# An mLSTM scan with its feed-forward on one core: scores of the first six chunks from each head's own 40 rows, in two halves of the array by turns, and a new list of first steps

## The chip, the cores and the metric

One NeuronCore of a Trainium2 chip. A kernel's time is the device time of one launch, in microseconds, the median of three runs. What is profiled is one execution of its own, whose time stands beside its span below.

## The reference, cut to what matters

```python
# q, k, v, o_gate: (4, 8, 768, 40); i_gate, f_gate: (4, 8, 768)
for t in range(S):
    m_new = maximum(f[t] + m, i[t]);  f_stab = exp(f[t] + m - m_new);  i_stab = exp(i[t] - m_new)
    C = f_stab * C + i_stab * outer(v[t], k[t])          # (40, 40) of each head
    n = f_stab * n + i_stab * k[t]
    y[t] = sigmoid(o_gate[t]) * (C @ q[t]) / maximum(abs(n . q[t]), 1.0)
x = y.transpose(0, 2, 1, 3).reshape(3072, 320)
h = x @ w_in                                             # (320, 2048)
g = maximum(h, 0) + alpha * minimum(h, 0)
out = g @ w_out                                          # (2048, 320)
```

## The kernel before, in words

The scan is done in chunks of 128 tokens, 24 in all (4 sequences of 6), with the 8 heads of a chunk together. A chunk's output is the sum of two products: its tokens among themselves, where the scores k.q of a head (128x128) are weighed with decays and multiplied with the values, and the state C of all earlier chunks, multiplied with q. Two chunks make a group of 256 tokens, on which the feed-forward runs: up with `w_in` (`ph`, lines 738 to 745), an activation, a split into a high and a low part (`gh`, `gl`), and down with `w_out` (`po`, line 775).

The first six chunks (`NDIR = 6`, one sequence) take another way than the rest: their products are float32. The step `qTn`/`kTn` turns q and k of a chunk by a transpose on TensorE into `pqk`, with two heads in one column block of 128: the even head of a pair in rows 0 to 39, the odd head in rows 64 to 103 (`R = 64 + D` = 104 rows). `qcn` copies q out of PSUM in one copy (`qf`, line 1034). `kcn` copies k twice, by `padded_copy`: rows 0 to 63 into the first half of `kf` (line 330), rows 64 to 103 into the second half (line 331). The other rows of both halves of the two `kf` tiles hold zeros, written once by the step `kfz` (`padded_tiles`, lines 319 and 320, GpSimd). The scores of the even heads (`sc n 0`) and of the odd heads (`sc n 1`) are then two steps of four matmuls each over all 104 rows, where the zeros take the other head out (`scores`, line 1102). `wg n par` weighs such a half with its decays on VectorE (`weigh`, line 1106), `v n` multiplies with the values (`values`, line 351), `fm n` is the product with the state (`pI`, line 412), `um n` the chunk's own addition to the state (`pu`, line 193).

Beside this the opening loads both weight matrices. Each comes as 64-bit words over SP's queue and is made into float32 on chip: the step `d` of a block issues the load (`wi`, `wr`, `wo`), `s`, `x`, `y`, `j` put the words together on ScalarE and VectorE (lines 834 to 858), `h`/`H` cast the high part on ScalarE and `k`/`K` on GpSimd (line 866), `l`/`L` take the low part on VectorE and `p` on GpSimd (line 870). Blocks are `i00` to `i31` (rows of `w_in`), `r0`, `r2` (its last 64 rows) and `o0` to `o7` (`w_out`). `warm2` issues two matmuls of 256 columns whose result nobody reads (`dense`, line 166).

What sets the order of all this is the string `ORDER`: names of steps, run one after the other; `pin` then ties every instruction behind the one that was issued before it on its engine, so no scheduler moves anything. `dqn`, `dvn`, `don`, `dLn` in it issue the loads of q and k, v, the output gate and the decays. After the names of `ORDER` come those of `PATTERN`, group by group, to the end; `U`, `R`, `S`, `G`, `K`, `D` are the steps of a feed-forward piece (up, relu, activation, high, low, down).

Transposes, scores and updates take their PSUM tiles by turns from four buffers (`psa`); the first chunks' scores borrow the feed-forward's.

Of the kernel before, what the change touches and what calls it, by code (L numbers as in the profile page):

```python
# [17 lines left out]
def kernel(ctx: ExitStack, tc: tile.TileContext, q, k, v, i_gate, f_gate, o_gate, w_in, w_out, alpha, out):  # L18
    nc = tc.nc
# [6 lines left out]
    halves = slice(0, P // 2), slice(P // 2, P)  # L26
# [14 lines left out]
    turns = ["b", "a"]  # L41

# [270 lines left out]
    kpads = []  # L313
# [328 lines left out]
    def row_of(g, fp, e):  # L642
# [302 lines left out]
    def first_group():  # L945
# [78 lines left out]
        for j in range(2):  # L1024
            kpads.append(sb.tile([P, 2, 512], F32, tag="kS", name=f"kf{j}", bufs=2))
# [67 lines left out]
        def scores(n, par):  # L1093
            if n >= GC:
                ps = psa(f"pS{n}_{par}")
            elif n * par == 0:
                ps = ps_h.tile([P, 512], F32, tag="h", name=f"pS{n}_{par}")
            else:
                ps = ps_o.tile([P, 512], F32, tag="o1", name=f"pS{n}_{par}")
# [97 lines left out]
        def decay_parts(k, tag):  # L1197
# [29 lines left out]
            kfz=padded_tiles, Cz=zero_states,  # L1227
# [5 lines left out]
        def values_of(n):  # L1233
            got["h", n] = values(n, [E[n, 0], E[n, 1]])
# [5 lines left out]
        def chunk_steps(n):  # L1240

            steps[f"wd{n}"] = lambda: weighed(n)
            steps[f"v{n}"] = lambda: values_of(n)
# [9 lines left out]
            for par in range(2):  # L1253
# [5 lines left out]
                steps[f"sc{n}{par}"] = lambda par=par: scores(n, par)  # L1259
# [115 lines left out]
```

## Time and profile before

| | |
|---|---|
| median of 3 runs | 455.18 us (455.04 to 455.19) |
| the profiled execution | 454.57 us |
| its span, first to last instruction | 452.7 us |
| PE busy | 445.0 us (98%) |
| DVE / ACT / POOL busy | 307.4 / 313.7 / 310.0 us |
| chain that ended last, by engine | PE 88%, ACT 3%, DMA 2%, DVE 2%, issue 2% |
| the six chunks' scores (line 1102), busy | 13.0 us in 96 instructions |

A float32 matmul shows as two instructions in the profile, so four matmuls of a score step are "x8". An instruction's time holds some 0.17 us in which the next one already runs; what a step costs the engine is read from the distance of two starts or from the chain of waits, where each piece is counted once. The opening is the stretch to about 113 us in which the first two groups' feed-forward is mixed with the chunks and the weights; behind it the order is that of `PATTERN`.

### The profile page before, as it was taken

Reading aid. Unit: us, or ns where it says so; the run is one execution under the profiler, and the core shown is the slowest. Engines: PE = TensorE matmul, PEld = TensorE weight load, DVE = VectorE, ACT = ScalarE, POOL = GpSimd, SP = SyncE. Lnnn points to the kernel's source line nnn. Section 1 sums busy time; section 2 is a strip of 40 time slices with the busy share of each in tenths; the row PEclk is TensorE's granted clock in tenths of the full one; section 3 lists DMA queues with packets and bytes.
Section 4 is the critical chain, followed back from the end, with each engine's and each line's share of the span. In section 5 each row is a group of like instructions: output and inputs, shape, how many; then the busy total and the mean of one; then the engine's idle time right before and its main releaser. Section 6 shows DMA issues by size and latency. Waiting matters only on the chain.

```text
span 452.7 us, 12026 instructions
## 1 busy us (share of the span) xinstructions
PE 445.0 (98%) x4560; PEld 433.4 (96%) x4560; DVE 307.4 (68%) x659; ACT 313.7 (69%) x717; POOL 310.0 (68%) x400
## 2 busy tenths in 40 slices
PE   8999999999999999999999999999999999999997
PEld 6779999999999999999999999999999999999996
DVE  4799999557866867767768767758758757753321
ACT  5999997858857867758858758659759658433331
POOL 7846366667879689588798698597798696143241
PEclk9999999999999999999999999999999999999999
DMA  8998996289875575596773774598572451000000
GB/s 186 220 261 204 284 237 203 52 165 225 183 162 113 134 167 109 129 178 165 152 165 96 134 177 104 112 192 178 128 179 77 98 140 41 2 30 0 30 1 29
DMA packets 156163, 61.61 MB, mean 136 GB/s; under 512 B 140154, under 2 KB 145834, under 8 KB 156106
## 3 DMA queue, kind: packets, MB, share of 16 engines
q1 hardware_dynamic: 156026, 60.75, 59.1%
q8 instruction: 36, 0.59, 0.5%
q14 instruction: 21, 0.17, 0.1%
q10 hardware_dynamic: 80, 0.11, 0.1%
HBM read 36.90 MB, written 4.03 MB: 90 GB/s over the span
## 4 chain that ended last, share of the span: by engine, by line
PE 88%; ACT 3%; DMA 2%; DVE 2%; issue 2%; POOL 1%; SPq 1%; POOLq 0%; DVEq 0%
PE po L775 36%; PE ph L738 5%; PE ph L743 5%; PE ph L739 5%; PE ph L740 5%; PE ph L745 5%; PE ph L741 5%; PE ph L742 5%; PE ph L744 5%; PE pH L392 4%; PE pS L494 4%; PE pu L193 1%; PE pI L418 1%; PE px L603 1%; DMA kn<-in_k_dram 1%
## 5 line engine op out<-in xcount | busy, mean ns | idle before, releaser
L764 POOL TENSOR_TENSOR gl<-g,gh 128x512 fp32r<-128x512 f32 x74 | 95.7, 1294 | 32.6 <-ACT gh L762 31.4
L775 PE MATMUL po<-OH,gh 128*128 128x320 f32 x368 | 111.5, 315 | 0.0
L748 ACT ACTIVATE g<-ph 128x512 f32<-128x512 f32 x96 | 57.4, 598 | 76.7 <-PE ph L745 74.8
L775 PE MATMUL po<-OL,gh 128*128 128x320 f32 x368 | 108.7, 308 | 0.0
L753 DVE SCALAR_TENSOR_TENSOR g<-g,oma,ph 128x256 f32<-128x256 f32 x148 | 63.6, 471 | 65.1 <-ACT g L748 65.0
L775 PEld LDWEIGHTS po<-OH,gh 128*128 128x128 f32 x368 | 69.2, 188 | 0.0
L775 PEld LDWEIGHTS po<-OL,gh 128*128 128x128 f32 x368 | 69.2, 188 | 0.0
L775 PE MATMUL po<-OH,gl 128*128 128x320 f32 x368 | 68.7, 308 | 0.0
L775 PEld LDWEIGHTS po<-OH,gl 128*128 128x128 f32 x368 | 57.5, 188 | 0.0
L738 PE MATMUL ph<-XH,WH 128*128 128x256 f32 x192 | 54.1, 282 | 0.3 <-ACT wi L844 0.3
L739 PE MATMUL ph<-XH,WH 128*128 128x256 f32 x192 | 53.3, 278 | 0.0
L743 PE MATMUL ph<-XL,WH 128*128 128x256 f32 x192 | 53.1, 277 | 0.1
L740 PE MATMUL ph<-XH,WL 128*128 128x256 f32 x192 | 53.2, 277 | 0.0
L745 PE MATMUL ph<-XL,W 128*128 128x256 f32 x192 | 53.1, 277 | 0.0
L741 PE MATMUL ph<-XH,WL 128*128 128x256 f32 x192 | 53.1, 277 | 0.0
L742 PE MATMUL ph<-XH,W 128*128 128x256 f32 x192 | 53.0, 276 | 0.0
L744 PE MATMUL ph<-XL,WH 128*128 128x256 f32 x192 | 53.0, 276 | 0.0
L377 ACT CAST E<-pS 128x512 bf16<-128x512 f32 x72 | 41.1, 582 | 15.1 <-DVE pS L374 15.1
L465 ACT ACTIVATE E<-Lb,gates 128x128 f32<-128x128 f32 x160 | 50.0, 392 | 0.0
L762 ACT CAST gh<-g 128x512 fp32r<-128x512 f32 x74 | 45.7, 618 | 4.0 <-PE po L775 2.4
L738 PEld LDWEIGHTS ph<-XH,WH 128*128 128x128 f32 x192 | 36.0, 188 | 0.6 <-ACT wi L844 0.4
L450 POOL TENSOR_TENSOR og<-og,r 128x320 f32<-128x320 f32 x18 | 13.0, 724 | 34.3 <-DVE r L443 32.8
(200 smaller groups left out, 1126.1 us busy)
## 6 DMA issues: line engine op xcount, KB each, us to landing
Lb<-L_d SPq DMA_DIRECT2D x20, 512.0 KB
wo<-in_moe_w_out_dram SPq DMA_DIRECT2D x8, 640.0 KB
wi<-in_moe_w_in_dram SPq DMA_DIRECT2D x8, 512.0 KB
qn<-in_q_dram SPq DMA_DIRECT2D x24, 160.0 KB
kn<-in_k_dram SPq DMA_DIRECT2D x24, 160.0 KB
og<-in_o_gate_dram SPq DMA_DIRECT2D x24, 160.0 KB
va<-in_v_dram SPq DMA_DIRECT2D x24, 160.0 KB
out_dram<-ob SPq DMA_DIRECT2D x11, 320.0 KB
```

The source lines that it names most:

```text
L738: nc.tensor.matmul(dst, WH[half][:, 0, hs], XH[:, 0], start=True, stop=False)
L739: nc.tensor.matmul(dst, WH[half][:, 1, hs], XH[:, 1], start=False, stop=False)
L740: nc.tensor.matmul(dst, WL[half][:, 0, hs], XH[:, 0], start=False, stop=False)
L741: nc.tensor.matmul(dst, WL[half][:, 1, hs], XH[:, 1], start=False, stop=False)
L742: nc.tensor.matmul(dst, W2[:, fs], XH[:, 2], start=False, stop=False)
L743: nc.tensor.matmul(dst, WH[half][:, 0, hs], XL[:, 0], start=False, stop=False)
L744: nc.tensor.matmul(dst, WH[half][:, 1, hs], XL[:, 1], start=False, stop=False)
L745: nc.tensor.matmul(dst, W2[:, fs], XL[:, 2], start=False, stop=True)
L748: nc.scalar.activation(gt, ph, AF.Relu, scale=-1.0)
L753: nc.vector.scalar_tensor_tensor(out=y[:, e], in0=gt[:, e], scalar=oma[:, f : f + 1], in1=ph[:, e], op0=ALU.mult, op1=ALU.add)
L764: (nc.vector if split else nc.gpsimd).tensor_tensor(gl, y, gh.bitcast(F32), ALU.subtract)
L775: nc.tensor.matmul(po[j], x[:, e, j * P : (j + 1) * P], W[f // NB][:, f % NB], **ends)
```

## The change

The scores of a chunk become one step `scn`. Each of its matmuls reads only the 40 rows of one head: rows 0 to 39 of `qf` and `kf` for the even head of a pair, rows 64 to 103 for the odd one, and the two alternate, pair by pair, into two PSUM tiles. In the built program those matmuls have a tile of 64x128 of the array, at row 0 and at row 64; before they had 128x128. `kf` needs no zeros: `kfz`, `padded_tiles` and `padded_copy` go, and `kcn` is one copy of 104 rows as `qcn` is. `ORDER` is written anew: 20 steps `warm2` more (90 filling matmuls in place of 50), the casts `i00h`, `r0h`, `o2h`, `i30h`, `o7h` now on GpSimd (`k`), `i11k` now on ScalarE (`h`), `o7l` on GpSimd (`p`), and most names at other places. The steps from `PATTERN` are as before. A loop that only reserved buffers a second and a third time goes as well.

```diff
-    def padded_tiles():
-        for K in kpads:
-            nc.gpsimd.memset(K[64:R, 0], 0.0)
-            nc.gpsimd.memset(K[:64, 1], 0.0)
...
-    def padded_copy(K, pk):
-        nc.scalar.copy(K[:64, 0], pk[:64])
-        nc.scalar.copy(K[64:R, 1], pk[64:R])
...
-    ORDER = """warm14 dq0 Cz warm2 warm2 warm2 qT0 warm2 sca0 lf0a kT0 i00d lf0z lf0b li0 L0 sca1 bj0 dq1 warm2 qc0 lqa lqb kc0
+    ORDER = """warm14 dq0 Cz i00d qT0 lf0z sca0 dq1 lf0a warm2 lf0b warm2 L0 warm2 lqa dv0 sca1 i00s warm2 warm2 kT0 sp01 warm2
...
+        keys = [sb.tile([P, 2, 512], F32, tag="kS", name=f"kf{j}", bufs=2)[:, 0] for j in range(2)]
...
             if j == 0:
-                qk[n] = sb.tile([P, 512], F32, tag="qf", name=f"qf{n}"), padded(n)
-                copy(qk[n][j][:R], pq[:R])
-            else:
-                padded_copy(qk[n][j], pq)
+                qk[n] = sb.tile([P, 512], F32, tag="qf", name=f"qf{n}"), keys[(n + NDIR) % 2]
+            copy(qk[n][j][:R], pq[:R])
...
-        def scores(n, par):
-            if n >= GC:
-                ps = psa(f"pS{n}_{par}")
...
+        def scores(n):
+            for par in range(2):
+                if n >= GC:
+                    ps = psa(f"pS{n}_{par}")
...
+                pS[n, par] = ps
             for p in range(NPR):
                 sl = slice(p * P, (p + 1) * P)
-                nc.tensor.matmul(ps[:, sl], qk[n][1][:R, par, sl], qk[n][0][:R, sl], start=True, stop=True)
-            pS[n, par] = ps
+                for par in range(2):
+                    r = slice(64 * par, 64 * par + D)
+                    nc.tensor.matmul(pS[n, par][:, sl], qk[n][1][r, sl], qk[n][0][r, sl], start=True, stop=True)
...
+            steps[f"sc{n}"] = lambda: scores(n)
```

Three places of the new order, as the built programs have it. First TensorE, at chunk 3, between the first down step of group 0 (`po`) and the values of chunk 3 (`pH`); `pu` is a chunk's addition to the state. Before:

```order
L775 MATMUL po_1_789<-OH_103,gl_0_735 128x320
L1102 MATMUL pS_1_805<-qf_578,kf_157 128x128 x4
L412 MATMUL pI_825<-C_85,qf_802 64x84 x8
L1102 MATMUL pS_1_840<-qf_802,kf_156 128x128 x4
L193 MATMUL pu_845<-va_81,kd_731 40x42 x8
L1102 MATMUL pS_0_856<-qf_802,kf_156 128x128 x4
L351 MATMUL pH_871<-va_82,E_0_691 64x42 x8
L351 MATMUL pH_871<-va_82,E_1_737 64x42 x8
```

And now:

```order
L193 MATMUL pu_815<-va_82,kd_747 40x42 x8
L1088 MATMUL pS_0_829<-qf_576,kf_149 128x128
L1088 MATMUL pS_1_830<-qf_576,kf_149 128x128
...
L1088 MATMUL pS_0_829<-qf_576,kf_149 128x128
L1088 MATMUL pS_1_830<-qf_576,kf_149 128x128
L193 MATMUL pu_840<-va_81,kd_759 40x42 x8
L335 MATMUL pH_854<-va_82,E_0_670 64x42 x8
L335 MATMUL pH_854<-va_82,E_1_768 64x42 x8
L1088 MATMUL pS_0_887<-qf_811,kf_148 128x128
```

Both halves of chunk 3's scores now stand together, with one update (`pu`) between them and the values that need both; before, three other steps and chunk 4's scores stood between the second half and those values.

Second VectorE, between the normalizer of chunk 0 (`r`, from `pH`) and the low part of the first feed-forward input (`XL`). Before:

```order
L443 RECIPROCAL r_489<-r_489 128x8
L856 SCALAR_TENSOR_TENSOR t_wo_474<-t_wo_474,wo_337 128x640
L448 SCALAR_TENSOR_TENSOR og_308<-og_308,r_489 128x320
L1106 TENSOR_TENSOR E_0_482<-pS_0_497,E_0_482 128x512
L870 TENSOR_TENSOR W_76<-t_wr_353,W_76 64x512
L452 TENSOR_TENSOR xn_488<-pH_451,og_308 128x320
L423 TENSOR_TENSOR T_563<-pI_507,gates 128x336
L1238 TENSOR_TENSOR T_413<-T_413,pH_529 128x336
```

And now:

```order
L427 RECIPROCAL r_546<-r_546 128x8
L841 SCALAR_TENSOR_TENSOR t_wo_472<-t_wo_472,wo_339 128x640
L432 SCALAR_TENSOR_TENSOR og_278<-og_278,r_546 128x320
L436 TENSOR_TENSOR xn_545<-pH_474,og_278 128x320
L407 TENSOR_TENSOR T_556<-pI_508,gates 128x336
L855 TENSOR_TENSOR W_76<-t_wr_344,W_76 64x512
L1223 TENSOR_TENSOR T_398<-T_398,pH_522 128x336
```

The weighing of chunk 2's even heads (`E_0_482`) has left this piece; it now stands behind the second `xn`.

Third SP's queue, from the load of `wr` (the last 64 rows of `w_in`) to that of k of chunk 2. Before:

```order
L824 DMA wr_273<-in_moe_w_in_dram 64x1024 x2
L141 DMA og_308<-in_o_gate_dram 128x8x40 x2
L125 DMA va_81<-in_v_dram 128x8x40 x2
L824 DMA wi_1_317<-in_moe_w_in_dram 128x1024
L112 DMA qn_77<-in_q_dram 128x8x40
L112 DMA kn_79<-in_k_dram 128x8x40
L907 DMA wo_337<-in_moe_w_out_dram 128x2x640
```

And now:

```order
L125 DMA va_81<-in_v_dram 128x8x40 x2
L809 DMA wr_254<-in_moe_w_in_dram 64x1024 x2
L809 DMA wi_1_264<-in_moe_w_in_dram 128x1024
L141 DMA og_278<-in_o_gate_dram 128x8x40 x2
L892 DMA wo_339<-in_moe_w_out_dram 128x2x640
L112 DMA qn_77<-in_q_dram 128x8x40
L112 DMA kn_79<-in_k_dram 128x8x40
```

q and k of chunk 2 now come behind the 640 KB of `wo`, and the values ahead of `wr`.

## Rows read from the trace of the kernel before

**Rows 1.** The page: busy time of TensorE, its slices beside those of VectorE, ScalarE and the DMA engines, and the shares of the chain that ended last.

```profile
PE 445.0 (98%) x4560; PEld 433.4 (96%) x4560; DVE 307.4 (68%) x659; ACT 313.7 (69%) x717; POOL 310.0 (68%) x400
PE   8999999999999999999999999999999999999997
DVE  4799999557866867767768767758758757753321
ACT  5999997858857867758858758659759658433331
DMA  8998996289875575596773774598572451000000
PE 88%; ACT 3%; DMA 2%; DVE 2%; issue 2%; POOL 1%; SPq 1%; POOLq 0%; DVEq 0%
```

**Rows 2.** Busy time of each engine in four stretches (us from the span's start, length): PE, PEld, DVE, ACT, POOL (instructions), then the granted clock of TensorE, the DMA engines' share, GB/s.

```profile
0.00:5.00 5.00, 4.16 (x20) 3.02 (x21) 1.49 (x6) 1.28 (x1) 4.16 (x23) 1.00 0.69 139
15.00:20.00 5.00, 4.71 (x59) 3.85 (x57) 3.75 (x10) 4.46 (x10) 4.88 (x7) 1.00 0.94 242
35.00:75.00 40.00, 39.37 (x487) 37.13 (x486) 38.14 (x78) 37.88 (x79) 23.26 (x26) 1.00 0.93 256
45.00:50.00 5.00, 4.92 (x84) 4.44 (x84) 4.86 (x10) 4.92 (x9) 2.86 (x3) 1.00 0.90 229
```

**Rows 3.** The chain of waits in order of time (start, length, engine and step): pieces of it between 39 and 60 us.

```profile
39.14 0.73 PE pI L412 x16
39.87 1.09 PE pS L1102 x8
...
41.40 0.44 PE pu L193 x16
...
44.17 0.89 PE pS L1102 x8
...
45.80 1.09 PE pS L1102 x8
...
47.32 1.10 PE pS L1102 x8
...
59.01 0.59 ACT kf L330
59.61 0.58 ACT kf L331
```

**Rows 4.** TensorE's timeline (start, length, instructions; in brackets the idle time before and what ended it): the filling matmuls at the start and at 8 us, chunk 2's q transpose, the later gates' transposes, the values of chunk 0, the first up step of group 0, chunk 5's scores, the first up step of group 1.

```profile
0.84 4.43 PE L166 MATMUL warm<-const-bfloat16-1.0 128*128 128x256 bf16 x20 [0.84 <-PEq L1359]
5.06 0.98 PE L274 MATMUL pqk<-ident,qn 128*104 128x128 f32 x4
...
8.15 0.84 PE L166 MATMUL warm<-const-bfloat16-1.0 128*128 128x256 bf16 x6
...
18.26 0.65 PE L274 MATMUL pqk<-ident,qn 128*104 128x128 f32 x4
...
21.18 0.55 PE L1017 MATMUL ps_g_all<-ident,g_WH 96*128 96x96 f32 x4
...
24.00 1.13 PE L351 MATMUL pH<-va,E 128*64 128x42 f32 x32 [0.48 <-DVE gates L1021]
...
32.97 0.39 PE L738 MATMUL ph<-XH,WH 128*128 128x256 f32 x1
...
64.33 1.95 PE L1102 MATMUL pS<-qf,kf 104*128 104x128 f32 x16
...
67.24 0.36 PE L738 MATMUL ph<-XH,WH 128*128 128x256 f32 x1 [0.32 <-ACT wi L844]
```

**Rows 5.** Groups of instructions by line and form (count, busy us, mean ns of one, idle before): ScalarE's copies of k and its cast of a piece of `w_in`, and the weighing on VectorE.

```profile
L331 ACT COPY kf<-pqk 40x512 f32<-40x512 f32 x6 | 3.5, 580 | 0.1
L866 ACT CAST WH<-t_wi 128x512 fp32r<-128x512 f32 x7 | 4.3, 636 | 0.1
L1106 DVE TENSOR_TENSOR E<-pS,E 128x512 f32<-128x512 f32 x12 | 8.0, 679 | 1.2 <-PE pS L1102 1.1
```

**Rows 6.** GpSimd's and VectorE's timelines: the last of the four writes of zeros (`kfz`), the step behind it, and the sums `L` for which that step waits too.

```profile
15.22 0.52 POOL L320 MEMSET kf<- 64x512 f32 x1
15.71 1.39 POOL L1223 TENSOR_TENSOR g_WH<-g_li,g_L 32x512 f32<-32x512 f32 x1
13.50 1.21 DVE L1158 TENSOR_TENSOR_SCAN g_L<-g_WL,g_lf 32x512 f32<-32x512 f32 x1
```

**Rows 7.** SP's timeline, and one row of VectorE's: the issue of `wr` for the second half of `w_in`, the weighing of chunk 2's even heads with its wait; and ScalarE's first reading of that `wr`.

```profile
40.87 1.11 SPq L824 DMA_DIRECT2D wr<-in_moe_w_in_dram  x2
27.13 0.69 DVE L1106 TENSOR_TENSOR E<-pS,E 128x512 f32<-128x512 f32 x1 [0.25 <-PE pS L1102]
49.18 0.69 ACT L834 ACTIVATE t_wr<-wr 128x512 f32<-128x512 f32 x1
```

**Rows 8.** Who waited for whom, TensorE to 115 us: one row.

```profile
PE pS L494 <- DMA kS<-kS: 0.4, 1, 0.4
```

More of the change, by code (lines that the diff above doesn't have):

```diff
@@ L25 @@
     NPR = H // 2
-    halves = slice(0, P // 2), slice(P // 2, P)
     GC = 2
@@ L41 @@
     turns = ["b", "a"]
+    halves = slice(0, P // 2), slice(P // 2, P)
     settled = []
@@ new lines @@
+    ORDER = """warm14 dq0 Cz i00d qT0 lf0z sca0 dq1 lf0a warm2 lf0b warm2 L0 warm2 lqa dv0 sca1 i00s warm2 warm2 kT0 sp01 warm2
+        warm2 warm2 warm2 li0 warm2 bj0 qT1 qc0 lqb lqc kc0 bTt wt0 eeL lqd warm2 lf1a bTc i00y lqe warm2 qc1
+        warm2 r0d ex01 lf1b ewj i01d warm2 warm2 warm2 sp11 do0 ex11 wTt sp00 wTc L1 warm2 sp10 ex00 li1 ex10
+        kT1 warm2 eel warm2 bj1 warm2 wd0 wtl warm2 warm2 gma warm2 o0d dq2 og1 r0s gmd sc0 um0 uc0 eTt eTc gmm
+        wd1 kc1 alT wg01 alC warm2 i00j lpa ewl fm1 warm2 ft1 sc1 gmc warm2 lpb i00k qT2 wg00 lpc warm2 r0y wg11
+        qc2 lpd dv1 glt um1 uc1 i01s kT2 i01x warm2 wg10 lpe kc2 i00p sp20 r0j dL warm2 o0s v0 o0x glc i11d sp21
+        ex20 warm2 fm2 i01j warm2 r0k i01h v1 ex21 i01p gr0 o0j gg0 gx0 i11x i11s ft2 r0l warm2 dq3 qT3 o1d gp0
+        ta1 warm2 wd2 qc3 x0 gr1 sc2 gg1 gx1 warm2 wg20 gp1 warm2 r0H o0h warm2 xa0 i11j dL4 x1 xa1 dq4 i10d xd1
+        xd0 kT3 i11h F0 warm2 kc3 U00 sq30 o0l r0L ex40 wg21 R00 ey30 v2 S00 o1s ta2 o1y um2 i10x warm2 i10s
+        sq31 o2d uc2 i20d U01 kT4 wd3 fm3 i10j wd4 gr2 G00 ey31 ex41 K00 o1j qT4 ft3 i10h dv2 D00 i11l R01 do1
+        qc4 i20s um3 S01 uc3 sc3 kc4 um4 wg30 wg31 o1h o1l og2 v3 i20x gg2 G01 o5d o2x i10p i20j i20h uc4 sc4
+        gx2 i21d K01 ta3 i20p wg40 o5s r2d o2s o2j gr3 dq5 fm4 wg41 o5x U02 o2k o2l r2x ft4 r2s o5j gg3 v4 gp2
+        gx3 dL5 gp3 qT5 R02 o4d U03 i21s qc5 r2j S02 ex50 R03 r2H x2 i21y r2h o3d ta4 xa2 G02 dq6 i21j r2L D01
+        S03 i21h fm5 kT5 i31d r2p x3 kc5 ft5 dv3 dL7 o4s K02 xd2 i21p D02 G03 do2 o4y i30d K03 o3s o3y xa3 wd6
+        o3j U04 V05 o4j ex51 R04 S04 sc5 o3h o7d o3p r05 o4h G04 i31x xd3 i31s s05 o4p um6 uc6 wg51 K04 F1 o6d
+        wg50 U10 U11 R10 gr4 og3 S10 gg4 gx4 R11 S11 v5 G10 o5h G11 o5p K10 vp0 K11 D10 i30x ta5 U12 i31j dL6
+        gr5 i31h U13 R12 gg5 D11 i31l o7x gx5 S12 gp5 i30s G12 i30j K12 R13 i30k dq7 do3 gp4 D12 g05 o6x i30l
+        o7s tp0 S13 G13 o6s U06 o7j x4 K13 tp1 D13 U07 R06 tp2 N05 R07 o6j xa4 D03 x5 D04 o7k D05 S06 vp1 o6h
+        o7p G06 xa5 S07 o6l xd5 tp3 xd4 K06 D06 G07 K07 D07 Z0"""
@@ L970, in first_group @@
         for tag, width, bufs in (("gl", 512, 3), ("t", 2 * DM, 3), ("g", 512, 3), ("gh", 512, 3), ("ob", 2 * DM, 1)):
-            for _ in range(bufs):
-                late_pool.tile([P, width], U32, tag=tag, name=f"at_{tag}", bufs=bufs)
+            late_pool.tile([P, width], U32, tag=tag, name=f"at_{tag}", bufs=bufs)
         make_identity(nc, ident)
@@ L1091, in first_group @@
         pS = {}
[L1093 to L1099 removed]
+        def scores(n):
+            for par in range(2):
+                if n >= GC:
+                    ps = psa(f"pS{n}_{par}")
+                elif n * par == 0:
+                    ps = ps_h.tile([P, 512], F32, tag="h", name=f"pS{n}_{par}")
+                else:
+                    ps = ps_o.tile([P, 512], F32, tag="o1", name=f"pS{n}_{par}")
+                pS[n, par] = ps
             for p in range(NPR):
                 sl = slice(p * P, (p + 1) * P)
[L1102 to L1103 removed]
+                for par in range(2):
+                    r = slice(64 * par, 64 * par + D)
+                    nc.tensor.matmul(pS[n, par][:, sl], qk[n][1][r, sl], qk[n][0][r, sl], start=True, stop=True)
         def weigh(n, par):
@@ L1258, in chunk_steps @@
                 add(f"ex{n}{par}", lazily(lambda par=par: decay(n, par)))
-                steps[f"sc{n}{par}"] = lambda par=par: scores(n, par)
                 steps[f"wg{n}{par}"] = lambda par=par: weigh(n, par)
```

24 lines of the change are left out of this document (1 added, 23 removed).

## The prediction

> **What bounds the kernel now.** I read the page first. TensorE is busy 98% of the span and makes 88% of the chain that ended last [rows 1]; its slices are full from the second to the last but one, while VectorE, ScalarE and the DMA engines are full only in the first six or seven, that is to about 75 us. So the kernel has two parts: an opening in which four resources are about equally full, and a long rest that is TensorE work alone. The change touches only the opening. What is won there comes off the total one for one, because the rest is the same row of instructions behind it; what is taken off another engine in the opening is worth something only where TensorE waits for it.
>
> Next the busy time by stretches [rows 2]. From 35 to 75 us TensorE is busy 39.37 of 40 us, ScalarE 37.88, VectorE 38.14, and the DMA engines have a share of 0.93. Then the chain of waits [rows 3]: from 39 to 48 us it runs through TensorE's own steps, among them score steps of 0.89 to 1.10 us; at 59 us it runs through ScalarE's two copies of k. TensorE's timeline [rows 4] gives the marks: the first up step of group 0 begins at 32.97, the first of group 1 at 67.24.
>
> **Scores.** A half's score step costs 0.89 to 1.10 us [rows 3], chunk 5's two together 1.95 [rows 4]. 0.89 us for 8 instructions is 111 ns for 128 columns. No row shows two instructions in the upper and lower rows of the array. The nearest rows are those that split its columns: the product with the state takes 0.73 us for 16 instructions of 84 columns, whose halves alternate [rows 3]. At 111 ns for 128 columns these would take 16 x 73 = 1.17 us one after the other; so the halves run beside each other. 16 score instructions, two at a time, are 8 x 111 = 0.89 us; the state product has 0.73 - 16 x 73/2 = 0.15 us on top, and I add that: 1.04 us for a whole chunk, against 1.99 for chunk 3 (1.09 + 0.89), 2.19 for chunk 4 and 1.95 for chunk 5: 6.13 before, 3.12 now, 3.0 us less. Bounds: no overlap, nothing less; perfect overlap without the 0.15, 3.5 less. Chunks 0 to 2 shrink as much, but stand before 33 us, where TensorE fills its time with matmuls that nobody reads.
>
> The Trainium skill speaks against this term ("TensorE: Matmul & The Clock Gate", LDWEIGHTS): the time of a weight load follows its columns and not its rows, so loading 40 rows costs what 104 did. By that rule, if loads go one after another, the sum would keep the scores' old price; it is the first rival below.
>
> **Filling matmuls.** 40 more. At 8 us six take 0.84 us, of which some 0.17 are the last one's tail: 0.115 us each [rows 4], 4.6 us in all. All but one `warm2` stand before the first up step, where they lie in TensorE's waits; the one behind costs 0.23 us. Without that cover they would cost all of it.
>
> **A wait added.** Both halves now end together, and the values of chunk 3 stand behind them with one update between (the first of the three places in the order). VectorE needs 2 x 0.68 us to weigh [rows 5], the update covers 0.44 [rows 3]: TensorE waits 0.92 us. Chunks 4 and 5 have an up step or more between. Behind the waiting values stand chunk 4's scores and the next up step, all in TensorE's own queue.
>
> **ScalarE, to 33 us.** Three copies of k go (0.58 each) and two casts go to GpSimd (`i00`, `r0`, 0.64 each) [rows 5]: 3.0 us, the upper bound of what the first up step can gain; the lower is nothing. What else ends there is SP's queue and VectorE. q and k of chunk 2 now come behind 640 KB of `wo`: at 242 GB/s [rows 2] 2.7 us. Its transpose ran at 18.26 without waiting, so it can now begin at up to 20.9; right behind it stand the later gates' transposes, which ran at 21.18 and on which the values of chunk 0 hung (0.48 us waited, 24.00) [rows 4]. Against this the writes of zeros go from GpSimd: the step behind them can begin with the sums' end at 14.71 in place of 15.71 [rows 6], 1.0 us. So the values of chunk 0 come between 0 and 1.0 us sooner; I take 0.5. From there VectorE's row leads to the feed-forward's input (second place in the order); the weighing of chunk 2 goes out of it, 0.69 us and its wait of 0.25 [rows 7], 0.94 us. Together 1.4 us at the first up step, nearer the middle of 0 and 3.0 than either end.
>
> **From the first up step to 67 us.** TensorE: 3.0 less, 0.23 and 0.92 more: 1.85 us. ScalarE loses three copies there, 1.74 us, and exchanges casts one for one (`o2` out, `i11` in); with its 2.1 us idle from 35 to 75 it can follow. VectorE loses nothing and has 40 - 38.14 = 1.86 us idle in that stretch [rows 2], which this just fills; so I take 1.7. Bounds: a loss of 1.15 (scores no faster), a gain of 2.8 (no wait at chunk 3's values).
>
> **After that** TensorE's work is what it was. The output gate's six loads of the second sequence now go ahead of the first transposes on SP; a wait of 0.4 us for `kS` could go [rows 8], so 0 to 0.4, taken as 0. The casts that go to GpSimd there (`i30`, `o7`) cost nothing as long as they lie beside TensorE's down steps, 0.6 us each if not.
>
> **Sum.** 1.4 + 1.7 = 3.1 us, from 454.57 of the profiled execution to 451.5. The median is 0.61 above that execution, so 452.1. Ends: all upper bounds, 3.0 + 2.8 + 0.4 = 6.2, 449.0; all lower, 456.3.
>
> **Rivals.**
> *The halves don't overlap.* For it: no row shows row halves, and column halves load weights into different columns, which these don't. Against it: the state product's price. Then the 3.0 us fall away: 1.4 - 0.23 - 0.92 = 0.25 us gained, 454.9. Chance 0.14. The rule named above leads here.
>
> *The loads are late.* The DMA engines' share of 0.93 [rows 2] leaves little to move forward. The place: the second `wr`, issued at 40.87 and read at 49.18 by ScalarE [rows 7], now comes behind another 512 KB of `w_in`, 2.2 us at 229 GB/s [rows 2], while ScalarE comes there 3 us sooner. If it landed less than 5 us before it was read, ScalarE stands, with the next relu of the feed-forward behind it. Price: up to the 1.7 us of that stretch, 453.8, and at more than one place nothing is left. Chance 0.12, half of it counted as no change.
>
> *TensorE's clock rises late: slower.* The first 20 fillers take 0.22 us each, the lower level, 1.2 GHz; those at 8 us 0.115, the upper, 2.4 GHz [rows 4]; the granted clock reads 1.00 in every stretch, the first included [rows 2], so here the durations tell the level. Now 14 fillers end near 3.9 us, and TensorE idles up to 1.1 us until q of chunk 0 has landed (its transpose began at 5.06). 32 fillers stand between it and the second decay row. Should the rise wait until then, these cost 32 x 0.105 = 3.4 us and the transposes and rows among them some 2.1 more: the front comes 5.5 us late, in all 2.4 slower, 457.6. It decides from about 3.1 us, that is when more than about 30 of the fillers run slow, hence rarely. Chance 0.08. A further 0.04 for scores whose weight loads lie open, each like the 0.2 us by which a step of 1.09 stands over one of 0.89 [rows 3].
>
> **How the numbers follow.** The forecast has 0.62. 0.2%, 0.9 us, is about what a measurement of this kernel can tell from no change. Faster: 0.62 and half of the late loads, 0.68. Same: 0.14 and the other half, 0.20. Slower: 0.08 + 0.04 = 0.12. The forecast's own range is 449.2 to 453.6; with the first two rivals and the worst sum it goes to 456.0, which leaves the slow clock out, some 0.15 in all.
>
> **What would show it.** Right: the two score tiles' instructions start in pairs, a chunk's scores take 1.0 to 1.1 us, the first up step begins near 31.6 and group 1's near 64.1, and TensorE waits near 0.9 us for chunk 3's weighing. Wrong: score instructions 110 ns apart; a ScalarE wait for `wr`; fillers of 0.2 us beyond 6 us; VectorE with waits of more than 2 us between 35 and 65, which would mean that it was no cap.

## The result: 0.7% slower, not 0.7% faster

The changed kernel took 457.57 us, the median of 13 runs; the kernel before, beside it on the same chip, 455.08. The ratio of the runs is 1.0067, 95% interval 1.0053 to 1.0082. The forecast was 452.1 us with a range of 449.2 to 456.0: the time lies outside, on the slower side. The profiled execution took 457.69 us, its span is 456.0 against 452.7.

The marks first. TensorE's timeline of the kernel after, beside [rows 4]; a number in brackets is idle time and what ended it:

```profile
5.08 2.10 PE L166 MATMUL warm<-const-bfloat16-1.0 128*128 128x256 bf16 x10
...
21.34 0.60 PE L274 MATMUL pqk<-ident,qn 128*104 128x128 f32 x4
...
24.83 1.13 PE L335 MATMUL pH<-va,E 128*64 128x42 f32 x32 [0.44 <-ACT kf L1017]
...
33.08 0.36 PE L723 MATMUL ph<-XH,WH 128*128 128x256 f32 x1
...
43.66 1.16 PE L1088 MATMUL pS<-qf,kf 40*128 40x128 f32 x16
46.79 0.51 PE L193 MATMUL pu<-va,kd 128*40 128x42 f32 x16 [1.98 <-issue]
47.74 1.94 PE L335 MATMUL pH<-va,E 128*64 128x42 f32 x32 [0.44 <-DVE E L1091]
49.62 2.08 PE L1088 MATMUL pS<-qf,kf 40*128 40x128 f32 x16
51.63 1.39 PE L396 MATMUL pI<-C,qf 104*64 104x84 f32 x16
52.94 0.58 PE L723 MATMUL ph<-XH,WH 128*128 128x256 f32 x1
...
70.53 0.36 PE L723 MATMUL ph<-XH,WH 128*128 128x256 f32 x1 [0.36 <-DVE g L738]
```

Group 0's first up step begins at 33.08 us, 0.11 later than before; group 1's at 70.53, 3.29 later. The span is 3.3 us longer, so nearly all of the loss lies between these two marks, and the rest is the same row of work. A whole chunk's scores, 16 instructions, show 1.16 us, as the eight of one half did before (45.73). But behind those of chunk 3 TensorE stands 1.98 us ("issue": the profile names nothing that ended it) and 0.44 us, and then everything is slow: the values of chunk 3 take 1.94 us for the 1.13 of chunk 0's [rows 4], the next scores 2.08 for 1.16.

The stretches say why these are slow (columns as in [rows 2]; the third number from the end is the granted clock):

```profile
40.00:45.00 5.00, 4.82 (x66) 4.14 (x64) 4.93 (x7) 3.18 (x10) 4.12 (x5) 1.00 0.53 84
45.00:50.00 5.00, 2.76 (x52) 2.59 (x53) 4.92 (x11) 4.13 (x7) 1.26 (x2) 0.78 1.00 296
50.00:55.00 5.00, 5.00 (x43) 4.59 (x42) 4.92 (x12) 3.96 (x6) 2.88 (x4) 0.54 0.98 210
```

From 45 to 50 us TensorE is busy 2.76 us, before 4.92 [rows 2], and from there on its granted clock is 0.78 and then 0.54: it has fallen from the upper level (2.4 GHz) to the lower (1.2 GHz) and is back at 1.00 from 55. VectorE is busy 4.92 to 4.93 us in all three. Ahead of the gap the DMA engines have a share of 0.53.

The chain of waits around the gap, beside [rows 3], where it ran through TensorE's own steps:

```profile
41.60 0.69 DVE gl L749
42.30 0.78 DVE t_wo L843
43.08 0.42 DVE T L407
43.49 1.98 DVE WL L855
45.47 0.41 DVE ph L738
...
46.99 0.70 DVE E L1091
47.74 1.94 PE pH L335 x32
```

It is on VectorE: the weighing of chunk 3 (`E`), for which the values wait, stands behind the low part `i11l` (`WL`), an activation (`ph`) and a state update (`C`). The low part is one long piece, 1.98 us. VectorE and GpSimd in their timelines there:

```profile
43.41 2.05 DVE L855 TENSOR_TENSOR WL<-t_wi,WH 128x512 fp32r<-128x512 f32 x1
...
42.37 1.32 POOL L218 TENSOR_TENSOR C<-C,gamB 104x336 f32<-104x336 f32 x1
43.66 1.26 POOL L855 TENSOR_TENSOR WL<-t_wi,WH 128x512 fp32r<-128x512 f32 x1
```

Before, the same step of the same size took 0.68 us:

```profile
39.56 0.68 DVE L870 TENSOR_TENSOR WL<-t_wi,WH 128x512 fp32r<-128x512 f32 x1
```

Now GpSimd runs two two-operand steps beside it, one right after the other, and VectorE's low part ends at 45.46, 0.54 us after the second of them (43.66 + 1.26 = 44.92).

So this is the theory B that the experiments test: VectorE comes late by a step that GpSimd stretches (this part is called G), TensorE stands, and the clock that falls then costs more than the wait. Its rivals: A, ScalarE's queue (the update `um4` needs a PSUM tile that ScalarE's copy of k, `kc4`, empties, and this copy stands behind a conversion that waited 2.37 us); C, matmuls of 40 rows lower the clock by themselves; D, the fillers in the front (the stretch up to the first up step).

### The profile page after: what moved, and what is told of

Its sections match the earlier page's. It is cut to its first block, busy times and chain, and to the rows that moved or that the text cites. A ratio compares the mean times of both kernels' runs of the same rounds, so it can differ in the third digit from the quotient of the medians.

```text
span 456.0 us, 12105 instructions
## 1 busy us (share of the span) xinstructions
PE 447.3 (98%) x4600; PEld 434.6 (95%) x4600; DVE 309.8 (68%) x658; ACT 307.8 (67%) x707; POOL 311.9 (68%) x401
## 4 chain that ended last, share of the span: by engine, by line
PE 92%; DVE 4%; ACT 2%; issue 1%; DMA 1%; SPq 0%; ACTq 0%; DVEq 0%
PE po L760 36%; PE ph L723 5%; PE ph L728 5%; PE ph L724 5%; PE ph L725 5%; PE ph L730 5%; PE ph L729 5%; PE ph L726 5%; PE ph L727 5%; PE pH L376 4%; PE pS L478 4%; PE warm L166 2%; PE pI L402 1%; PE px L587 1%; PE pu L193 1%; PE pS L1088 1%
## 5 line engine op out<-in xcount | busy, mean ns | idle before, releaser
L749 POOL TENSOR_TENSOR gl<-g,gh 128x512 fp32r<-128x512 f32 x74 | 95.7, 1295 | 32.2 <-ACT gh L747 31.0
L728 PEld LDWEIGHTS ph<-XL,WH 128*128 128x128 f32 x192 | 36.2, 189 | 0.3 <-DVE XL L580 0.3
```

Source lines behind the costliest of these rows:

```text
L728: nc.tensor.matmul(dst, WH[half][:, 0, hs], XL[:, 0], start=False, stop=False)
L749: (nc.vector if split else nc.gpsimd).tensor_tensor(gl, y, gh.bitcast(F32), ALU.subtract)
```

## Experiments

All ran beside the kernel before; the ratios are to it, with 95% intervals. Where the list has a line less, line numbers are one or two lower than in the kernel after (L1087 is L1088 there); in e4a, e13 and e17 code was added too. The kernel after has 1.0067.

| run | median us | ratio | interval |
|---|---|---|---|
| e1, ScalarE's copy first | 458.28 | 1.0076 | 1.0048 to 1.0104 |
| e7, low part early | 454.44 | 0.9989 | 0.9976 to 1.0001 |
| e2, gap filled | 455.40 | 1.0023 | 0.9997 to 1.0048 |
| e3, halves not by turns | 460.74 | 1.0147 | 1.0110 to 1.0184 |
| e9, e7 and `wr` early | 454.41 | 0.9978 | 0.9967 to 0.9990 |
| e10, e9 with fewer fillers | 457.76 | 1.0056 | 1.0031 to 1.0082 |
| e11, `i10p` moved, GpSimd unchanged | 458.50 | 1.0078 | 1.0049 to 1.0107 |
| e14, `i10p` behind a GpSimd step | 455.70 | 1.0023 | 1.0000 to 1.0047 |
| e15, e9 with chunk 2's q first | 457.07 | 1.0043 | 1.0026 to 1.0060 |
| e4a, list of before, 40 rows | 461.14 | 1.0129 | 1.0108 to 1.0149 |
| e13, e4a with zeros | 459.27 | 1.0091 | 1.0075 to 1.0108 |
| e17, e13 with fillers | 460.58 | 1.0101 | 1.0057 to 1.0146 |

**e1: is it ScalarE's queue?**

```diff
-qc4 i20s um3 S01 uc3 sc3 kc4 um4
+qc4 kc4 i20s um3 S01 uc3 sc3 um4
```

> The changed kernel with one step moved on ScalarE: the copy of chunk 4's k (kc4) stands ahead of the weight conversion i20s instead of behind it. In the changed kernel the update um4 needs the PSUM tile that this copy empties, and the copy stood behind i20s, which waited 2.37 us for a staging tile. Theory A (ScalarE's row and the PSUM tile hold TensorE): um4 no longer waits, TensorE's gap of 2.4 us between 44.8 and 47.7 us shrinks below 0.7 us, the granted clock stays at 1.00, 453 to 454 us. Theory B (VectorE's row is late, above all by the low-part step i11l of 2.05 us before the weighing of chunk 3): um4 goes early, but the values v3 then wait 2 to 3 us for the weighing, the granted clock of TensorE still falls below 0.9 between 45 and 55 us, 456.8 to 458 us.

TensorE's timeline:

```profile
44.71 0.51 PE L193 MATMUL pu<-va,kd 128*40 128x42 f32 x16
47.64 1.94 PE L335 MATMUL pH<-va,E 128*64 128x42 f32 x32 [2.43 <-DVE E L1090]
```

The update went early and the values waited 2.43 us for VectorE, as long as the two waits together had been; the clock fell as well (0.73 from 45 to 50 us). A is out.

**e7: VectorE's low part elsewhere.**

```diff
-ex40 wg21 R00
+ex40 wg21 i11l R00
...
-dv2 D00 i11l R01
+dv2 D00 R01
```

> The changed kernel with one step moved on VectorE: the low part i11l goes from behind the first down step's place (it began at 43.4 us, between the activation of group 0 and the weighing of chunk 3) to right behind the weighing of chunk 2's odd heads (wg21). Nothing is left out. Theory B (VectorE is late there and TensorE's idle time then lowers its clock): the gap before chunk 3's values shrinks from 2.4 us to about 1 us, the granted clock stays at 1.00 between 45 and 55 us, the values take 1.1 us in place of 1.94 and the next scores 1.1 in place of 2.1; 452.5 to 454.5 us. Rival D (the 2 us lost are already lost in the front, by the filling matmuls ahead of the first up step): the first up step stays at 33.1 us and the total moves by less than 1 us, 456.5 to 458 us. Theory C (40-row matmuls lower the clock by themselves): the clock falls all the same, 456 us or more.

Stretches and TensorE's timeline:

```profile
45.00:50.00 5.00, 3.87 (x80) 3.39 (x75) 4.96 (x10) 4.17 (x8) 3.23 (x3) 1.00 1.01 294
50.00:55.00 5.00, 4.10 (x59) 3.88 (x58) 4.64 (x10) 2.49 (x6) 1.60 (x3) 1.00 1.08 186
```

```profile
45.69 1.26 PE L335 MATMUL pH<-va,E 128*64 128x42 f32 x32 [0.48 <-DVE E L1090]
...
53.52 0.61 PE L274 MATMUL pqk<-ident,qn 128*104 128x128 f32 x4 [0.90 <-DMA qn<-in_q_dram]
```

One step moved gives 3.1 us back (457.57 to 454.44; 0.8% by the ratios). The wait for the weighing is 0.48 us, the clock stays at 1.00, and group 0's first up step is where it was (33.02). The low part itself, now at 36.19 with no two-operand step of GpSimd beside it, takes 0.68 us. That is B, and against C and D, each by itself, as causes of these 3 us. New waits appear, as for chunk 5's q; so it is still no faster than before.

**e2: is it the idle time or the clock?** 22 matmuls that add zero to group 0's output while TensorE would stand:

```diff
-sc3 kc4 um4 wg30 wg31 o1h o1l og2 v3
+sc3 kc4 fill18 um4 wg30 wg31 o1h o1l og2 fill4 v3
...
+                for _ in range(int(name[4:])):
+                    nc.tensor.matmul(ffs[0].po[0][:, : 2 * P], zero, x, start=False, stop=False)
```

> The changed kernel with 22 filling matmuls (zeros by ones, 256 columns, added into the first down step's accumulator, so the sums stay as they are): 18 before chunk 4's update um4 and 4 before chunk 3's values v3. They take up the time in which TensorE stood idle and nothing else is moved. 18 fill about 2 us at the upper clock. Theory B, second half (the idle time of 2.4 us lowers the granted clock, and this costs more than the idle time itself): the granted clock stays at 1.00 between 45 and 55 us, the first up step of group 0's third piece starts 3 us earlier than 53.0, 453.5 to 455 us. Rival C (it is the 40-row score matmuls that lower the clock): the clock falls as before between 45 and 55 us, 457 us or more. Rival E (clock back, but VectorE is the bound from there on): clock 1.00, and yet the total is within 1 us of 457.6.

The stretch of the gap:

```profile
45.00:50.00 5.00, 4.35 (x81) 3.55 (x81) 4.88 (x12) 4.66 (x9) 2.06 (x3) 1.00 0.93 262
```

455.40 us, 2.2 less than the kernel after, with useless work added and VectorE as late as before. The clock holds at 1.00. So of what e7 won about half is the clock's (by the ratios 0.44% of 0.78%, each ratio known to 0.13 to 0.26%), the rest the wait's. It came out 0.4 us above what I had given for B.

**e3: are the scores' turns worth anything?** All four matmuls of the even heads first, then those of the odd.

```diff
-            for p in range(NPR):
...
-                for par in range(2):
...
+            for par in range(2):
...
+                for p in range(NPR):
```

> The changed kernel with each chunk's scores in another order: the four matmuls of all even heads (rows 0 to 39) first, then the four of all odd heads (rows 64 to 103). The same instructions, but no two neighbours in different halves of the array. If the halves overlap only by turns, a chunk's scores take 1.9 to 2.1 us in place of 1.09. If TensorE's time for the scores is what the change wins from 35 to 67 us: 3 chunks x 0.9 = 2.7 us more, 459.5 to 460.5 us. If TensorE waits for VectorE there and the scores' time is hidden: 457 to 458 us. A third way: while scores take longer, TensorE is not idle long enough for its clock to fall; then 454 to 456.5 us.

TensorE's timeline, chunk 3:

```profile
44.54 1.71 PE L1088 MATMUL pS<-qf,kf 40*128 40x128 f32 x16
```

The total is 3.2 us more than in the kernel after. A chunk's scores take 1.71 us in place of 1.16 (less than I had thought; where the halves meet some probably still overlap), and the first up step begins 0.8 us later. Part of the 3.2 us is again the clock: it read 0.50 and 0.58 from 50 to 60 us, where the kernel after was back at 1.00 from 55, and chunk 4's scores took 3.10 us there. So the turns stand on the path and are worth less than 3.2 us at the upper level: 0.55 us a chunk.

**e11 and e14: does GpSimd stretch VectorE's step?** First e11, then e14:

```diff
-o5d o2x i10p i20j i20h uc4 sc4
+o5d o2x i20j i20h i10p uc4 sc4
...
-o5d o2x i10p i20j i20h uc4 sc4
+o5d o2x i20j i20h uc4 i10p sc4
```

> The changed kernel with one step moved on GpSimd: the low part i10p, which began at 43.66 us and took 1.26, goes behind the loads and casts that follow chunk 3's values, to about 47.9 us. VectorE's own row is as in the changed kernel: its low part i11l begins at 43.4 and took 2.05 us there, against 0.69 where GpSimd ran no two-operand step. Theory G (VectorE's step is slowed while GpSimd runs a two-operand step beside it): with GpSimd's addition to the state alone still beside it (42.4 to 43.7), i11l takes 1.0 to 1.4 us, the weighing of chunk 3 comes 0.7 to 1.1 us sooner, TensorE's idle time shrinks to about 1.5 us; the total is 1 to 3.5 us less, by whether the clock then holds. Rival (i11l is long for another reason, a wait for its data or its place): it takes 1.9 to 2.1 us again and the total is within 0.7 us of 457.6.

In e11 `i10p` passed no other step of GpSimd, so GpSimd's order was the old one: the low part began at 43.43 and took 2.05 us, as if nothing had been done. This tells nothing of G and stands as a second run of the kernel after. e14 moved it one step further.

> The changed kernel with the low part i10p on GpSimd behind the next addition to the state (in e11 it was moved past no other GpSimd instruction, so that GpSimd's order stayed what it was). Now only the state step of 42.4 to 43.7 us stands beside VectorE's low part i11l. Theory G: i11l takes 0.8 to 1.3 us in place of 2.05, chunk 3's weighing comes 0.7 to 1.2 us sooner, TensorE's gap before the values shrinks to 1.2 to 1.7 us; if the clock holds, 453.5 to 455 us, if it falls all the same 456 to 457. Rival (i11l is long by itself): 2.0 us again, 457 to 458.5.

VectorE, GpSimd and TensorE in their timelines of e14:

```profile
42.67 0.82 DVE L854 TENSOR_TENSOR WL<-t_wi,WH 128x512 fp32r<-128x512 f32 x1
...
46.23 1.59 DVE L854 TENSOR_TENSOR OL<-t_wo,OH 128x640 fp32r<-128x640 f32 x1
...
41.62 1.32 POOL L218 TENSOR_TENSOR C<-C,gamB 104x336 f32<-104x336 f32 x1
...
45.85 1.28 POOL L854 TENSOR_TENSOR WL<-t_wi,WH 128x512 fp32r<-128x512 f32 x1
...
44.81 0.51 PE L193 MATMUL pu<-va,kd 128*40 128x42 f32 x16 [0.71 <-issue]
45.76 1.27 PE L335 MATMUL pH<-va,E 128*64 128x42 f32 x32 [0.44 <-DVE E L1090]
...
49.54 1.39 PE L396 MATMUL pI<-C,qf 104*64 104x84 f32 x16 [1.42 <-POOL xn L436]
```

VectorE's step, its data and its neighbours on VectorE are the same; with one GpSimd step less beside it, it takes 0.82 us in place of 2.05. That is G, shown. It ends 0.55 us after the GpSimd step that is left (41.62 + 1.32 = 42.94). 1.9 us are won. But `i10p` now runs beside VectorE's next low part (`OL`), which takes 1.59 us, against 0.82 in the kernel after (48.20): the stretch has moved. VectorE's `og` stands behind it, GpSimd's `xn` waits 1.16 us for `og`, and TensorE waits 1.42 us for `xn`, after which the clock fell in this execution (456.81 us). Runs with a granted clock of 0.998 or more took 454.0 to 455.3.

**e9: the loads that VectorE held.** In the kernel after SP stood 3.3 us for a buffer that VectorE's joining of `wo` frees, and `wr`, chunk 5's q and the decays `Lb` stood behind it; hence the share of 0.53. To the edit of e7 comes:

```diff
-R01 do1 qc4
+R01 do1 r2d qc4
...
-wg40 o5s r2d o2s
+wg40 o5s o2s
```

> The changed kernel with two steps moved: the low part i11l early on VectorE as in e7, and on SP's queue the load of the second wr (r2d) ahead of the load of wo (o5d) that waits for VectorE from 39.6 to 43.1 us. In the changed kernel and in e7 that wait held wr, chunk 5's q and k and the decays Lb behind it; wr was issued at 45.3 instead of 40.9 us, Lb landed at 56.3 to 56.5 instead of 53.4, and in e7 TensorE waited 0.9 us for q of chunk 5 and 0.6 to 0.8 us for the output that hangs on Lb. Theory F (the loads held in SP's queue are the next bound): the DMA engines' share from 40 to 45 us rises from 0.56 to above 0.75, Lb lands near 54.3, both waits of TensorE go, 1.0 to 1.8 us less than e7: 452.6 to 453.5 us. Rival (VectorE is the bound between 40 and 68 us, the loads only look late): within 0.5 us of e7, 454.0 to 454.9 us.

VectorE, GpSimd and TensorE in their timelines:

```profile
56.89 1.78 DVE L854 TENSOR_TENSOR W<-t_wr,W 64x512 fp32r<-64x512 f32 x1
...
56.85 1.28 POOL L854 TENSOR_TENSOR W<-t_wr,W 64x512 fp32r<-64x512 f32 x1 [0.53 <-POOL E L452]
...
60.78 0.86 PE L759 MATMUL po<-OH,gl 128*128 128x320 f32 x4 [1.10 <-DVE gl L748]
```

The share from 40 to 45 us rose to 0.88 and TensorE's wait for q of chunk 5 is gone, but by the ratios the total is only 0.1% under e7, which the intervals don't tell from nothing: the rival. A later wait is VectorE's again: another low part begins beside a GpSimd step and takes 1.78 us; TensorE waits 1.10 us for what stands behind it. At 0.9978 this is the best version found, 1.0 us under the kernel before.

**e10: fewer fillers.** e9 without 15 `warm2`: 6 ahead of `sc0`, 4 of `sp11`, 2 of `qT1`, 3 of `kT0`.

> As e9, and 30 of the 40 added filling matmuls of the front taken out (6 warm2 before the scores of chunk 0, 4 before the second half of its decays, 2 and 3 further ahead). In the changed kernel chunk 2's q landed at 19.4 us and was transposed at 21.3, behind 15 groups of fillers that stand in the chain of waits; ScalarE stood 2.1 us for it and the first up step began at 33.1. Theory D (the fillers stand on the path of the front): the q transpose of chunk 2 comes at 20.0 to 20.4, the first up step at 31.6 to 32.3, the total 0.8 to 1.5 us under e9. Rival (the front hangs on the loads or on VectorE, the fillers lie in waits): the first up step stays at 32.8 to 33.2 and the total within 0.4 us of e9. Second rival (without the fillers TensorE's clock stays at its lower level in the front): fillers and transposes before 15 us take twice as long, the first up step after 34, the total 1 us or more above e9.

```profile
15.00:20.00 5.00, 4.04 (x46) 2.48 (x42) 2.97 (x10) 3.83 (x9) 3.74 (x5) 0.71 1.02 234
20.00:25.00 5.00, 5.00 (x48) 4.42 (x49) 2.28 (x5) 1.76 (x4) 3.11 (x4) 0.61 0.88 190
```

In these stretches the granted clock is 0.71 and 0.61 (1.00 in the kernel after), the first up step begins at 34.71, and the total is 3.4 us over e9. That is the second rival: without these fillers the clock falls in the front of this list.

**e15: chunk 2's q ahead of chunk 1's scores**, on top of e9.

```diff
-warm2 ft1 sc1 gmc warm2 lpb i00k qT2
+warm2 ft1 qT2 sc1 gmc warm2 lpb i00k
```

> As e9 (low part i11l and the load of wr early), and on TensorE the transpose of chunk 2's q ahead of chunk 1's scores in place of behind them. In the changed kernel q of chunk 2 had landed at 19.4 us, TensorE came to it at 21.3 and ScalarE stood 2.1 us for it; the filling matmuls can't be taken out without losing the clock (e10). Theory H (ScalarE's relief was lost to TensorE's place of that transpose): ScalarE copies q at 20.7 to 21.0 instead of 22.0, its wait falls to about 1 us, the first up step comes 0.6 to 1.2 us sooner than in e9 and the total is 0.5 to 1.2 us under e9: 453.2 to 453.9. Rival (the path to the first up step goes through VectorE and GpSimd, the gates' transposes follow the scores anyway): within 0.4 us of e9, 454.0 to 454.8.

ScalarE's and TensorE's timelines:

```profile
19.88 0.59 ACT L1016 COPY qf<-pqk 104x512 f32<-104x512 f32 x1 [0.65 <-PE pqk L274]
...
28.88 0.62 PE L274 MATMUL pqk<-ident,qn 128*104 128x128 f32 x4 [0.93 <-issue]
...
30.89 1.16 PE L1087 MATMUL pS<-qf,kf 40*128 40x128 f32 x16 [0.85 <-DVE T L1222]
```

ScalarE had q 2.1 us sooner than in the kernel after (22.03) and 1.5 sooner than in e9 (21.38), and yet the first up step began at 33.61, against 32.41 in e9 and 32.2 to 33.1 in the seven kernels with this front. Two waits of 0.9 us are new. H is wrong, and the rival's range is missed too: the median is 2.7 us over e9. The profiled execution, with a granted clock of 0.998, took 455.07; runs with 0.996 or less took 456.2 to 458.7.

**e4a, e13, e17: the new scores in the old list.** Scores from 40 rows and one copy of k in the list of before, the halves as two steps at their old places; in e13 the four writes of zeros come back to GpSimd, into columns that nobody reads; in e17 nine `warm2` more. The diff is against the kernel after; `idle_zeros` is the step `kfz` of e13 and e17.

```diff
-        def scores(n):
+        def scores(n, par):
...
+            r = slice(64 * par, 64 * par + D)
+            nc.tensor.matmul(ps[:, sl], qk[n][1][r, sl], qk[n][0][r, sl], start=True, stop=True)
...
+        def idle_zeros():
+            for K in kpads:
+                nc.gpsimd.memset(K[64 : 64 + D, 1], 0.0)
+                nc.gpsimd.memset(K[:64, 1], 0.0)
```

> One part of the change alone: the kernel with the list of before (no zero writes, fillers as before), k copied once, the scores from each head's 40 rows, but the even and the odd half as two steps at their old places, so that no halves run side by side. What is left is the relief of ScalarE (six copies of 0.58 us) and GpSimd (2 us of zero writes before 15.7). If these bound the opening: 0.7 to 2 us less than before, 453.2 to 454.5 us. If TensorE and VectorE bound it: within 0.5 us of before, 454.7 to 455.7. If 40-row scores by themselves cost more (weight loads lying open or a lower clock): above 456.

VectorE, GpSimd and TensorE in their timelines of e4a:

```profile
14.92 1.75 DVE L841 SCALAR_TENSOR_TENSOR t_wi<-wi,t_wi 128x512 uint32<-128x512 uint32 x1
...
14.76 1.37 POOL L1203 TENSOR_TENSOR g_WH<-g_li,g_L 32x512 f32<-32x512 f32 x1 [1.56 <-DVE g_L L1138]
...
17.84 0.96 PE L1172 MATMUL pg<-g_gd,unit 32*104 32x192 f32 x2 [2.11 <-DVE g_gd L1165]
```

5.9 us slower than before, with less work on two engines: the third outcome in time, but not by the cost of a narrow matmul alone. The zeros gone, GpSimd begins its two-operand step a microsecond sooner [rows 6], now beside VectorE's joining, which takes 1.75 us for 0.67. TensorE waits 2.11 us for what is behind it, and its clock falls (0.65, then 0.50 until 30 us).

> As e4a (list of before, scores from 40 rows one half at a time, one copy of k), and GpSimd again writes the four pieces of zeros at their old place, now into columns that nobody reads. GpSimd's and VectorE's instructions are those of before, one for one. In e4a GpSimd, without the zeros, ran a two-operand step at 14.76 us and another at 16.20; beside them VectorE's joining of a weight block took 1.75 us in place of 0.67 and the spread of the gate decays 1.19 in place of 0.34, TensorE waited 2.11 us for it and its granted clock was at 0.50 to 0.65 from 15 to 30 us. Theory G (a VectorE step is slowed while GpSimd runs a two-operand step beside it, and not beside a write of zeros): with this useless work the joining takes 0.7 us again, the wait of 2.1 us goes, the granted clock stays at 1.00, 453 to 455.7 us, 5.5 to 8 us less than e4a. Rival C (40-row scores alone lower the clock or cost more): the clock still falls in the front, 458 us or more.

The same engines and two stretches of e13:

```profile
14.89 0.67 DVE L841 SCALAR_TENSOR_TENSOR t_wi<-wi,t_wi 128x512 uint32<-128x512 uint32 x1
...
15.06 0.52 POOL L1089 MEMSET kf<- 64x512 f32 x1
...
15.89 0.57 PE L1178 MATMUL pg<-g_gd,unit 32*104 32x192 f32 x2 [0.17 <-DVE g_gd L1171]
```

```profile
15.00:20.00 5.00, 4.83 (x40) 3.72 (x36) 2.99 (x8) 3.60 (x7) 4.27 (x6) 0.66 0.86 226
20.00:25.00 5.00, 5.00 (x38) 4.14 (x39) 2.36 (x6) 3.41 (x7) 2.81 (x3) 0.50 1.06 235
```

G again: beside writes of zeros the joining takes 0.67 us and the wait is 0.17; useless work makes it 1.9 us faster than e4a. But the clock falls all the same, behind a stretch in which TensorE waited 0.5 and 0.17 us and no more. TensorE's row is that of before, where the clock stayed at 1.00 [rows 2], but for the rows of the score matmuls, 104 then and 40 now; the other difference is ScalarE's second copy of k. So for this list C is what is left, by elimination. At 45 us the narrow matmuls don't lower the clock without the wait (e7); whether they help the wait to lower it there was not tested.

> As e13 (list of before, zeros written for nobody, scores from 40 rows one half at a time, one copy of k), and 18 filling matmuls more: 12 ahead of chunk 0's first scores, 2 each at three places between there and chunk 1's second half. In e13 VectorE was back to its durations of before and TensorE waited nowhere over 0.5 us, yet its granted clock fell to 0.50 to 0.66 between 15 and 25 us; before, with the same row of TensorE instructions but 104 rows in each score matmul, it stayed at 1.00. If it is the scores of 40 rows that let the clock fall there and fillers that hold it: the granted clock stays at 1.00, the first up step begins at 33 to 34.5 us in place of 36.5, 454.5 to 456.5 us, 3 to 5 us less than e13. If the clock falls for another reason: 0.5 to 0.7 again between 15 and 25 us, 459 us or more, since the fillers then only cost time.

```profile
20.00:25.00 5.00, 5.00 (x44) 3.85 (x38) 1.86 (x5) 2.90 (x6) 2.79 (x3) 0.51 1.06 235
```

The fillers did not hold the clock: it fell at 20 us, with TensorE busy 5.00 of 5.00 us. Two of six runs kept 0.999 or 1.000 and took 456.4 to 456.5 us, four had 0.984 to 0.989 and 459.9 to 462.1. In the front of the changed list taking fillers out lets the clock fall (e10); in this list putting them in does not surely hold it. Why, no run here tells.

## Why the prediction was wrong, step by step

**Scores: right.** 1.04 us per chunk were forecast, and the chain counts 1.09 for chunk 0's, as much as for one half before [rows 3]:

```profile
15.94 1.09 PE pS L1088 x16
```

Without the turns a chunk takes 0.55 us more (e3). The first rival, that the halves don't overlap, is out. The rule on weight loads in the Trainium skill ("TensorE: Matmul & The Clock Gate", LDWEIGHTS) says that a load's time goes by its columns and not by its rows. The traces agree on that: a load took 0.188 us with 40 rows and 0.192 with 104. What did not hold is the condition that loads go one after another, by which a chunk would have kept about 2 us: all 16 instructions take 1.16.

**Filling matmuls at nothing before the first up step: wrong.** They make 22.5% of the chain of the first 40 us. Chunk 2's q transpose ran at 21.34 (18.26 before), where I had it at up to 20.9. What they cost by themselves no run shows, since the clock falls without them (e10).

**A wait of 0.92 us at chunk 3's values: the step that failed.** 1.98 and 0.44 us were measured. The price of one weighing was right (0.70 and 0.65 us). With `i11l` out of the way the wait is 0.48 (e7), about half of the 0.92: the values of the even heads begin behind the first weighing, and the second runs beside them. What I left out is when VectorE would come to it: I priced the two weighings from the end of the scores, and did not lay VectorE's row there beside GpSimd's. A low part takes 0.68 us where GpSimd does something else; in the new list it is 2.05. The trace of before already held such a row, on VectorE and GpSimd:

```profile
27.85 1.26 DVE L870 TENSOR_TENSOR W<-t_wr,W 64x512 fp32r<-64x512 f32 x1
...
27.29 1.28 POOL L870 TENSOR_TENSOR WL<-t_wi,WH 128x512 fp32r<-128x512 f32 x1 [3.32 <-ACT WH L866]
```

This low part ended at 29.11, 0.54 us after GpSimd's step (28.57); the same form at 55.94, with GpSimd idle, took 0.69.

The prediction did not use a rule that bears on this. The Trainium skill ("SBUF — State Buffer", Who interferes with whom) says that a VectorE instruction with two inputs in SBUF contends with a GpSimd instruction that reads SBUF, and not with one that only writes it. The traces agree on both halves: 0.82 us against 2.05 (e14), and 0.67 beside writes of zeros against 1.75 beside a two-operand step (e13, e4a). VectorE's weighing, which has one input in PSUM, was never stretched: it takes 0.64 to 0.70 us in every run.

**ScalarE, 1.4 us up to the first up step: wrong.** 33.08 against 32.97. ScalarE's 3.0 us are really gone, but it spends 2.08 of them waiting for the q transpose behind the fillers (its copy at 22.03). The values of chunk 0, which I had 0.5 us sooner, came at 24.83, 0.83 us later than before, and waited 0.44 us for ScalarE's copy of k; from them to the up step it took 8.25 us in place of 8.97, so 0.7 of the 0.94 us of the second part is there. e15 took most of ScalarE's wait away and gained nothing, so what bounds the front stays open. Over the kernels with this front the mark lies between 32.2 and 33.1, so about half of the 1.4 us was there at best.

**1.7 us to group 1's first up step: wrong in sign.** I named VectorE as a cap on the gain and gave it no way to be a loss. Between the marks 3.2 us were lost: 2.4 of TensorE standing, then about 3 by steps at the lower clock (0.81 for the values, 0.92 for the scores, 0.59 for the state product, and seven up matmuls at 0.21 us for 0.12, some 0.65) and a filler, against the scores' 3.0 gained (the forecast's figure); the rest, 0.6 us, lies in small waits that I have not followed.

**After that, nothing: right**, 3.29 us at the mark and 3.3 at the end.

**The other rivals.** Late loads were there, from another place of SP's queue, and are worth 0.1% at most (e9 against e7). The clock was the rival on the slower side, and its 457.6 us is the time that came. But that clock was to rise late at the start. It did rise later than before, ten fillers from 5.08 on still taking 0.19 us each on the average, yet the first up step came only 0.11 us late, and what cost the time is a fall at 45 us. The number agrees by luck, the mechanism does not.

## What to carry to other kernels

A duration from a trace holds with the neighbours it had there. When a list is laid out anew, go through VectorE's steps that read both inputs from SBUF and see what GpSimd will run beside each, and treat work that is taken off GpSimd as a move of everything behind it. When TensorE is full 98% of the time and a change makes it wait two microseconds at one place, price the clock behind the wait too. Here the slow steps behind a wait of 2.4 us added about 3 us, and useless matmuls in the gap paid for themselves.

## What was not expected of the hardware

- A VectorE step of 512 columns with both inputs in SBUF that began while a GpSimd two-operand step ran ended 0.54 to 0.56 us after it: 45.46 and 44.92 here, 43.49 and 42.94 in e14, 58.67 and 58.13 in e9, 16.67 and 16.13 in e4a. Here it was held for two GpSimd steps in a row; in e9 and e4a it went between two, and no run tells what decides that. Where VectorE began first it kept its time and GpSimd's step grew: VectorE's joining at 49.33 of the kernel after took 0.69 us, and GpSimd's `xn`, begun at 49.50, took 1.19, against 0.82 at 48.86 of the kernel before. GpSimd's writes of zeros stretched nothing.
- Two matmuls of 40 rows in the upper and lower half of the array cost as much as one of 104 rows: 16 instructions in 1.16 us, as eight before, weight loads of 0.19 us each included.
- The granted clock fell with TensorE standing 2.4 us (0.54 behind it). In e13 and e17 it fell with hardly any wait at all; before, with the row of e13 but 104 rows in the score matmuls, it held.
